# Attention, Elu layer and experts on one core: query projections moved up, half of the key-value products in front of the transposes, and another pacing of the side streams

## The chip, the cores and the metric

The kernel runs on one core of one Trainium2 chip. The metric is the device time of one execution in microseconds (us). The time before is the median of three runs. Times inside an execution come from one profiled execution.

## The reference

Three layers follow each other: a linear attention, an Elu MLP and a mixture of four experts.

```python
# q, k, v: (4, 8, 576, 64); phi(x): proj = x @ w_phi; proj -= max|proj| over the features
#                            phi = [exp(proj), exp(-proj)]   (256 features)
kv  = einsum('bhsf,bhsd->bhfd', phi(k), v);  z = sum_s phi(k)
num = einsum('bhsf,bhfd->bhsd', phi(q), kv)
den = einsum('bhsf,bhf->bhs',  phi(q), z) + 1e-6
x   = (num / den) as (2304 tokens, 512)
h   = x @ w_in                       # 512 x 2048
x   = where(h > 0, h, exp(min(h, 0)) - 1) @ w_out
p   = domain_probs / sum(domain_probs)
out = sum_e p[:, e] * (relu(x @ w1[e]) @ w2[e])   # 4 experts, 512 x 1024 x 512
```

## The kernel before, in words

**Streams.** The attention is cut into 16 pairs of heads (4 batches, 4 pairs each). `pair(i)` is a Python generator that is stepped 11 times, and `attention()` steps up to three pairs in turn: a new one begins every 5 steps (`ATT_LAG`), so the second half of a pair runs beside the first half of the next one. A second generator, `weight_stream()`, prepares weights: 32 conversions of the first half of w_in and w_out in SBUF (the ring), 32 conversions of the second half that are written to DRAM, and after them the split weights of the next stage, which it calls phase -1.

**A pair, in the order of its matmuls (with the names of the tables below).** L233 projects the last 64 keys. `proj(kt)` (L216, 16 matmuls) projects the keys, and `guard` (L222 the maximum, L223 the subtraction, both on VectorE) writes kp0 and kp1. `kexp` (L226, L227, ScalarE) makes exp and exp of the negative. `proj(qt)` and two more guards write qd0 and qd1. `tpose` (L262) transposes the guarded queries, four blocks a call, alternately from qd0 and qd1, and `qexp` (L270) writes their exponentials to ew. `kv` (L255, L256) multiplies the exponentials of the keys with the values. kvw (L284) is the copy of the result. `den` (L319) gives the denominator, copied to dd (L320, ScalarE). A DMA on ScalarE's queue (L325) spreads it to dn, VectorE adds 1e-6 and inverts (L331, L332), a DMA on SyncE's queue writes rec (L333), and two more read it back broadcast as rb (L337). `num` (L309) gives the numerator nd. L340 on VectorE multiplies nd with rb, and `put_x` writes the halves xh (L293, ScalarE) and xl (L296, GpSimd), which the Elu layer reads.

**The next pair's inputs.** `load(i+1)` (L171 to L179, SyncE's queue) stands behind the first query guard: kq, wbd in the first pair, v, and behind these six raw weight blocks (`ring_load`, L376) as long as there are any of the 32 left. There is one kq buffer.

**The Elu layer.** Nine tiles t of 256 tokens, four units u. L518 to L520 are its first matmuls (12 before the first `slot()`), L547 to L549 its second. The first two tiles run interleaved in two halves (the part that the title calls two-half), t2 to t6 one after the other, t7 and t8 interleaved. The first tile needs the four pairs of batch 0, and t2 needs the four of batch 1. `slot()` is called four times a unit: it steps the attention by `rate` and the weights by `wrate`.

**What sets the order.** Each engine has one queue, run in order. A list scheduler fixes the queues ahead of the run by its own estimate of what is ready; the order of the code is only its priority. Steps that a generator emits earlier are thus offered earlier, and can still be placed behind others.

**Phase -1 and the experts.** The second half of the Elu layer (L645 to L647, L724 to L726) and the four experts (L645 to L749) make up the rest of the span, from 441.6 us on.

Of the kernel before, what the change touches and what calls it, by code (L numbers as in the profile page):

```python
# [43 lines left out]
ATT_LAG = 5  # L44
PRE = 1.2
RATE = 1.4
WRATE = 2
WHEAD = 5
CVB = 4
# [3 lines left out]
HEAD = 2  # L53
SEG = 2
ATE = 6
# [14 lines left out]
def attn_elu_moe_kernel(ctx: ExitStack, tc: tile.TileContext, kq_in, vv, w_phi, w_in, w_out, probs, w1, w2, out):  # L70
# [7 lines left out]
    def pool(name, bufs=1, stack=ctx, **kw):  # L78
        return stack.enter_context(tc.tile_pool(name=name, bufs=bufs, reuse_waits="tile", **kw))
# [104 lines left out]
    def bank(shape=(P, 512)):  # L184
        return psum[0].tile(list(shape), F32, tag="bank", name="bank")
# [9 lines left out]
    for i in range(2):  # L195
        t = a1.tile([P, 10, P], F32, name=f"vt{i}")
# [6 lines left out]
    def blocks(t, n):  # L203
        return t[:, :n * P].rearrange("p (n f) -> p n f", f=P)

    def pair(i):
        b, p = divmod(i, NP)
        kq, v = loaded.pop(i)
        kt, qt = kq[:, :512], kq[:, 640:]

        def proj(src):
            ps = [bank() for _ in range(2)]
            for t in range(4):
                for h in range(2):
                    r = slice(h * D, h * D + D)
                    PE.matmul(blocks(ps[h], 4)[:, t], src[r, t * P:(t + 1) * P], wbd[r, h], start=True, stop=True)  # L216
            return ps

        def guard(dst, ps, n):
            src = blocks(ps, n)  # L220
            mx = a1.tile([P, n, 1], F32, tag=f"mx{n}", name="mx", bufs=2)
            V.tensor_reduce(out=mx[:, :, 0], in_=src, op=ALU.max, axis=AX.X, apply_absolute_value=True)  # L222
            mark[0] = V.tensor_tensor(out=dst, in0=src, in1=mx.to_broadcast([P, n, P]), op=ALU.subtract).ins  # L223

        def kexp(d0, d1, src):
            A.activation(d0, src, ACTF.Exp)  # L226
            amark[0] = A.activation(d1, src, ACTF.Exp, scale=-1.0).ins  # L227
# [10 lines left out]
        yield  # L238
        kexp(kp[0][:, :, 0], kp[0][:, :, 1], kp[0][:, :, 1])
        guard(kp[1][:, :, 1], pk1, 4)  # L240
        yield
        kexp(kpm[:D, :, 0], kpm[:D, :, 1], md[:D])
        kexp(kp[1][:, :, 0], kp[1][:, :, 1], kp[1][:, :, 1])
        pq0, pq1 = proj(qt)
        guard(qd[0], pq0, 4)
        if i + 1 < B * NP:
            loaded[i + 1] = load(i + 1)
        yield
        guard(qd[1], pq1, 4)
        yield  # L250
        pk = bank((P, 4, P))

        def kv(h, c):
            for t in range(4):
                PE.matmul(pk[:, 2 * h + c], kp[h][:, t, c], v[:, 4 * h + t], start=(t == 0), stop=False)  # L255
            PE.matmul(pk[:, 2 * h + c], kpm[:, h, c], v[:, 8 + h], start=False, stop=True)  # L256

        def tpose(j):
            pt = bank()
            for t in range(2):  # L260
                for h in range(2):
                    PE.transpose(blocks(pt, 4)[:, 2 * h + t], qd[h][:, 2 * j + t], ident)  # L262
            return pt
# [3 lines left out]
        def qexp(ps, c0, n):  # L267
            src = ps[:, :512].rearrange("p (h s) -> p h s", h=2)[:, :, :n] if n > P else blocks(ps, 2)[:, :, P - n:]
            for c, sc in ((0, 1.0), (1, -1.0)):
                amark[0] = A.activation(ew[:, :, c, c0:c0 + n], src, ACTF.Exp, scale=sc).ins  # L270

        kvw = a1.tile([P, 4, P], F32, tag=("kvh", "kvl")[i % 2], name="kvw")
        qexp(tpose(0), 0, 256)
        kv(0, 0)
        kv(0, 1)
        yield
        qexp(tpose(1), 256, 256)
        pt = bank()
        for h in range(2):
            PE.transpose(pt[:, h * P:(h + 1) * P], md[:, h], ident)  # L280
        qexp(pt, 512, D)
        kv(1, 0)
        kv(1, 1)
        A.activation(kvw, pk, ACTF.Copy)  # L284
# [60 lines left out]
    def attention():  # L345
        live = []
        nxt = 0
        step = 0
        while nxt < B * NP or live:
            if nxt < B * NP and step % ATT_LAG == 0:  # L350
                live.append(pair(nxt))
                nxt += 1
            for g in list(live):
                if next(g, True):
                    live.remove(g)
                    done[0] += 1
                else:
                    yield
            step += 1
# [52 lines left out]
    ready = set()  # L412
# [82 lines left out]
    def need_w(key):  # L495
        while key not in ready:
            next(weights, None)
# [4 lines left out]
    HU = FP // 2  # L502
# [87 lines left out]
    def split_x(g, load_half, keep):  # L590
        xs = [None] * 7

        def put(k, d):
            xv = xb.tile([P, 2, 2, TC], F32R, tag="xv", name="xv", bufs=XV)
            A.activation(xv[:, 0], d, ACTF.Copy)  # L595
            on[XL[k]].tensor_tensor(out=xv[:, 1], in0=d, in1=f32(xv[:, 0]), op=ALU.subtract)  # L596
            if keep:
                SP.dma_start(xvd[g][k], f32(xv))
            xs[k] = xv

        def sub(d, x, y):
            V.tensor_tensor(out=d, in0=x, in1=y, op=ALU.subtract)

        b22 = load_half(g, 1, 1)
        b12 = load_half(g, 1, 0)
        b11 = load_half(g, 0, 0)
        yield
        t0 = xb.tile([P, 2, TC], F32, tag="xt", name="xt", bufs=1)
        put(0, b11)
        sub(t0, b22, b12)  # L610
        yield
        sub(b12, b12, b11)
        put(1, t0)
        b21 = load_half(g, 0, 1)
        yield
        put(6, b22)
        put(3, b12)
        yield
        sub(b22, b22, b12)
        put(2, b21)  # L620
        yield
        put(4, b22)
        sub(b21, b21, b22)
        put(5, b21)
        xcur[0] = g, xs
# [138 lines left out]
    def slot():  # L764
        quota[0] += rate[0]
        while quota[0] >= 1:
            quota[0] -= 1
            if done[0] < limit[0]:
                next(stream, None)
        wquota[0] += wrate[0]  # L770
        while wquota[0] >= 1:
            wquota[0] -= 1
            next(weights, None)

    wrate = [WHEAD]
    wquota = [0.0]
    quota = [0.0]
    rate = [0.0]
# [3 lines left out]
    def drive(unit):  # L782
        unit.l1(slot)
        pend.append(unit)
        if len(pend) > LAG:
            pend.pop(0).l2(slot)

    def order(tail):
        seq = [(t, u) for k in range(0, HU, SEG) for t in range(HEAD) for u in range(k, k + SEG)]
        return seq + [(t, u) for t in range(HEAD, NTS - tail) for u in range(HU)] + [(t, u) for u in range(HU) for t in range(NTS - tail, NTS)]  # L790
# [8 lines left out]
    for t, u in order(TAIL):  # L799
        if u == 0:  # L800
            goal = NP * ((TS * t + TS - 1) // S + 1)
            while done[0] < goal:
                next(stream)
            limit[0] = NP * (t // 2 + 2)
            rate[0] = RATE if t < ATE else 0.0
            if t == HEAD:
                wrate[0] = WSLOW
            if t == ATE:
                att.close()
                xb = pool("xb")  # L810
                wst[0] = pool("wst")
                cmp = pool("cmp")
                wrate[0] = WFAST
            if t == NTS - TAIL:
                nxt = split_x(0, x_att, False)
        need_w(("elu", u))
        drive(Elu(t, u))
        next(nxt, None)
    for _ in nxt:
        pass  # L820
    wrate[0] = WRATE
    need_w(("w1", -1, 0))
# [176 lines left out]
```

## Time and profile before

| | |
|---|---|
| time, median of 3 runs | 1403.98 us (1400.96 to 1405.23) |
| profiled execution | 1403.51 us |
| its span | 1401.4 us |
| mean clock granted to TensorE | 0.989 |
| busy: TensorE, weight loads, VectorE, ScalarE, GpSimd | 1360.0, 1235.3, 661.0, 603.3, 365.3 us |
| first matmul of the Elu layer, first of phase -1 | 88.3 us, 441.7 us |

The span is the time between the first and the last instruction of the trace; 2.1 us of the profiled execution lie outside it. TensorE is busy for 97% of the span. Its busy time depends on the granted clock, so a matmul at half clock counts twice the time. The first 88 us hold the four pairs of batch 0 with nothing of the Elu layer between them.

### The profile page before, as it was taken

Reading aid. Unit: us, or ns where it says so; the run is one execution under the profiler, and the core shown is the slowest. Engines: PE = TensorE matmul, PEld = TensorE weight load, DVE = VectorE, ACT = ScalarE, POOL = GpSimd, SP = SyncE. Lnnn points to the kernel's source line nnn. Section 1 sums busy time; section 2 is a strip of 40 time slices with the busy share of each in tenths; the row PEclk is TensorE's granted clock in tenths of the full one; section 3 lists DMA queues with packets and bytes.
Section 4 is the critical chain, followed back from the end, with each engine's and each line's share of the span. In section 5 each row is a group of like instructions: output and inputs, shape, how many; then the busy total and the mean of one; then the engine's idle time right before and its main releaser. Section 6 shows DMA issues by size and latency. Waiting matters only on the chain.

```text
span 1401.4 us, 22057 instructions
## 1 busy us (share of the span) xinstructions
PE 1360.0 (97%) x8408; PEld 1235.3 (88%) x8408; DVE 661.0 (47%) x1212; ACT 603.3 (43%) x1347; POOL 365.3 (26%) x433
## 2 busy tenths in 40 slices
PE   6889999999999999999999999999999999999998
PEld 5679788989999999999898888988888988889897
DVE  5667875664543757583433422324333334323232
ACT  4668656564545747473343442124321224321121
POOL 3448753221226102352202430003410014300000
PEclk9999999999999999999999999999999999999999
DMA  7533355431414131464614143343245241433521
GB/s 219 177 97 107 95 184 154 137 113 56 136 46 151 30 113 37 130 222 140 219 63 180 45 143 113 135 158 120 80 143 202 96 166 38 143 128 120 181 68 68
DMA packets 105337, 173.46 MB, mean 124 GB/s; under 512 B 33040, under 2 KB 50576, under 8 KB 105232
## 3 DMA queue, kind: packets, MB, share of 16 engines
q1 hardware_dynamic: 98224, 162.55, 35.8%
q10 hardware_dynamic: 7008, 9.51, 1.9%
q8 instruction: 66, 1.08, 0.3%
q14 instruction: 39, 0.32, 0.1%
HBM read 118.13 MB, written 53.81 MB: 123 GB/s over the span
## 4 chain that ended last, share of the span: by engine, by line
PE 86%; DMA 6%; DVE 3%; ACT 2%; issue 1%; POOL 1%; SPq 1%; DVEq 0%; ACTq 0%; POOLq 0%
PE bank L645 9%; PE bank L647 9%; PE bank L646 9%; PE bank L747 9%; PE bank L748 9%; PE bank L749 9%; PE bank L255 3%; PE bank L518 3%; PE bank L547 2%; PE bank L520 2%; PE bank L519 2%; PE bank L548 2%; PE bank L549 2%; PE bank L724 2%; PE bank L725 2%; PE bank L726 2%
## 5 line engine op out<-in xcount | busy, mean ns | idle before, releaser
L645 PE MATMUL bank<-xv,w 128*128 128x384 f32 x840 | 279.1, 337 | 4.0 <-DVE c L659 1.6
L646 PE MATMUL bank<-xv,w 128*128 128x384 f32 x840 | 282.1, 336 | 0.0
L647 PE MATMUL bank<-xv,w 128*128 128x384 f32 x840 | 278.5, 336 | 0.0
L747 PE MATMUL bank<-w,h 128*128 128x512 f32 x576 | 225.8, 395 | 2.3 <-ACT h L661 2.3
L748 PE MATMUL bank<-w,h 128*128 128x512 f32 x576 | 227.4, 395 | 0.0
L749 PE MATMUL bank<-w,h 128*128 128x512 f32 x576 | 202.6, 395 | 0.0
L477 POOL TENSOR_TENSOR w<-wst,w 128x256 fp32r<-128x256 f32 x100 | 78.8, 793 | 389.5 <-ACT w L476 264.0
L645 PEld LDWEIGHTS bank<-xv,w 128*128 128x128 f32 x840 | 157.8, 188 | 13.4 <-DVE c L659 2.6
L646 PEld LDWEIGHTS bank<-xv,w 128*128 128x128 f32 x840 | 158.0, 188 | 4.8
L647 PEld LDWEIGHTS bank<-xv,w 128*128 128x128 f32 x840 | 157.6, 188 | 0.0
L747 PEld LDWEIGHTS bank<-w,h 128*128 128x128 f32 x576 | 108.2, 188 | 25.1 <-ACT h L661 3.0
L662 DVE SCALAR_TENSOR_TENSOR h<-bank,h 128x384 fp32r<-128x384 f32 x144 | 76.9, 554 | 112.9 <-ACT h L661 112.7
L748 PEld LDWEIGHTS bank<-w,h 128*128 128x128 f32 x576 | 108.2, 188 | 23.0
L661 ACT ACTIVATE h<-bank 128x384 fp32r<-128x384 f32 x144 | 66.7, 489 | 141.7 <-PE bank L647 90.0
L749 PEld LDWEIGHTS bank<-w,h 128*128 128x128 f32 x576 | 107.5, 188 | 21.4 <-DVE h L662 0.3
L651 ACT ACTIVATE cmab<-bank 128x384 f32<-128x384 f32 x60 | 29.4, 490 | 182.9 <-PE bank L647 182.9
L596 POOL TENSOR_TENSOR xv<-xs,xv 128x768 fp32r<-128x768 f32 x24 | 45.9, 1916 | 185.9 <-ACT xv L595 179.5
L659 DVE TENSOR_TENSOR bank<-cm,bank 128x384 f32<-128x384 f32 x48 | 26.9, 561 | 126.5 <-PE bank L647 112.6
L518 PE MATMUL bank<-xh,w 128*128 128x256 f32 x288 | 84.1, 292 | 2.3 <-ACT xh L293 2.0
L547 PE MATMUL bank<-gh,w 128*128 128x256 f32 x288 | 84.5, 295 | 0.0
L519 PE MATMUL bank<-xl,w 128*128 128x256 f32 x288 | 81.3, 282 | 0.3 <-POOL xl L296 0.3
L548 PE MATMUL bank<-gl,w 128*128 128x256 f32 x288 | 81.5, 283 | 0.0
(116 smaller groups left out, 2601.2 us busy)
## 6 DMA issues: line engine op xcount, KB each, us to landing
xv<-xvd SPq DMA_DIRECT2D x42, 768.0 KB, 4.1
wst<-in_w SPq DMA_DIRECT2D x64, 256.0 KB, 2.7
xvd<-xv SPq DMA_DIRECT2D x21, 768.0 KB, 4.3
yscr<-y SPq DMA_DIRECT2D x54, 256.0 KB, 2.6
y<-yscr SPq DMA_DIRECT2D x54, 256.0 KB, 3.1
kq<-in_kq SPq DMA_DIRECT2D x16, 320.0 KB, 3.3
rb<-rec SPq DMA_DIRECT2D x32, 144.0 KB, 3.0
xscr<-nd ACTq DMA_DIRECT2D x16, 288.0 KB, 2.0
```

The source lines that it names most:

```text
L477: on[WL[v % len(WL)]].tensor_tensor(out=lo, in0=x, in1=f32(hi), op=ALU.subtract)
L518: PE.matmul(ph[:, j], w[:, 0, c], xh[:, kc], start=(kc == j == 0), stop=False)
L519: PE.matmul(ph[:, j], w[:, 0, c], xl[:, kc], start=False, stop=False)
L547: PE.matmul(o, w[:, 0, c], self.gh[:, j], start=start, stop=False)
L548: PE.matmul(o, w[:, 0, c], self.gl[:, j], start=False, stop=False)
L645: PE.matmul(o, hi[:, c], x[:, 0, kc], start=not more and kc == 0, stop=False, skip_group_check=more)
L646: PE.matmul(o, hi[:, c], x[:, 1, kc], start=False, stop=False, skip_group_check=more)
L647: PE.matmul(o, lo[:, c], x[:, 0, kc], start=False, stop=kc == 1, skip_group_check=more)
L662: V.scalar_tensor_tensor(out=h[:, 1], in0=c, scalar=0.0, in1=f32(h[:, 0]), op0=ALU.max, op1=ALU.subtract)
L747: PE.matmul(self.acc, h[:, 0, c], w[0], start=f == 0, stop=False)
L748: PE.matmul(self.acc, h[:, 0, c], w[1], start=False, stop=False)
L749: PE.matmul(self.acc, h[:, 1, c], w[0], start=False, stop=f == 2 * NQ - 1)
```

## The change

Four edits. (1) `proj(qt)` is emitted one step earlier, right behind the second key guard. (2) `kv(0, 0)` and `kv(0, 1)`, the products with kp0, are emitted ahead of the first `tpose`, behind the second query guard. The number of steps of a pair stays 11. (3) While t is 0 or 1, a slot steps the attention 2.0 times on average, not 1.4 times. (4) A slot doesn't step the weights while `wrate` is 5 and the last ring unit is converted. `wrate` is 5 (`WHEAD`) until t2 begins; it is 5.0 (`WFAST`) again from t6 to the end of the Elu layer, where `need_w` alone then steps the weights, all that are wanted at once.

```diff
+RHEAD = 2.0
...
         kexp(kp[0][:, :, 0], kp[0][:, :, 1], kp[0][:, :, 1])
         guard(kp[1][:, :, 1], pk1, 4)
+        pq0, pq1 = proj(qt)
         yield
         kexp(kpm[:D, :, 0], kpm[:D, :, 1], md[:D])
         kexp(kp[1][:, :, 0], kp[1][:, :, 1], kp[1][:, :, 1])
-        pq0, pq1 = proj(qt)
         guard(qd[0], pq0, 4)
...
         guard(qd[1], pq1, 4)
-        yield
         pk = bank((P, 4, P))
...
+
+        kv(0, 0)
+        kv(0, 1)
+        yield
 
         def tpose(j):
...
         qexp(tpose(0), 0, 256)
-        kv(0, 0)
-        kv(0, 1)
         yield
...
-        wquota[0] += wrate[0]
+        if wrate[0] != WHEAD or ("elu", HU - 1) not in ready:
+            wquota[0] += wrate[0]
...
-            rate[0] = RATE if t < ATE else 0.0
+            rate[0] = RHEAD if t < HEAD else RATE if t < ATE else 0.0
```

The lines of the changed kernel stand one higher from L216 on, four higher at L262 and two higher from L280 on.

**Place 1: TensorE, the third pair, before the Elu layer.** Before:

```order
L216 MATMUL bank<-wbd,kq 128x128 x8
L319 MATMUL bank<-ew,kvw 32x288 x8
L309 MATMUL bank<-ew,kvw 64x288 x8
L216 MATMUL bank<-wbd,kq 128x128 x8
L262 MATMUL bank<-ident,qd_506 128x128
L255 MATMUL bank<-vt_216,kp_503 128x128 x4
L256 MATMUL bank<-vt_216,kpm 128x128
L255 MATMUL bank<-vt_216,kp_503 128x128 x4
L256 MATMUL bank<-vt_216,kpm 128x128
```

The first L216 row is the keys' projection, the second the queries'; L319 and L309 belong to the pair before; kp_503 and kp_504 are kp0 and kp1, qd_506 and qd_507 are qd0 and qd1. Of the change:

```order
L217 MATMUL bank<-wbd,kq 128x128 x8
L321 MATMUL bank<-ew,kvw 32x288 x8
L217 MATMUL bank<-wbd,kq 128x128 x8
L311 MATMUL bank<-ew,kvw 64x288 x8
L255 MATMUL bank<-vt_216,kp_503 128x128 x4
L256 MATMUL bank<-vt_216,kpm 128x128
L255 MATMUL bank<-vt_216,kp_503 128x128 x4
L256 MATMUL bank<-vt_216,kpm 128x128
L255 MATMUL bank<-vt_216,kp_504 128x128
L266 MATMUL bank<-ident,qd_506 128x128
```

The queries' projection now stands ahead of the numerator, and the products with kp0 stand ahead of the first transpose.

**The same pair on VectorE.** Before:

```order
L222 TENSOR_REDUCE mx<-bank 128x4 x2
L223 TENSOR_TENSOR qd_506<-bank,mx 128x512
L331 TENSOR_SCALAR dn<-dn 128x9
L223 TENSOR_TENSOR qd_507<-bank,mx 128x512
L124 TENSOR_SCALAR pcs<-pcs 128x256
L332 RECIPROCAL dn<-dn 128x9
```

These are the query guards, with the L331 of the pair before between them. Of the change:

```order
L223 TENSOR_REDUCE mx<-bank 128x4 x2
L127 SCALAR_TENSOR_TENSOR top<-raw,pcs 128x256
L224 TENSOR_TENSOR qd_506<-bank,mx 128x512
L333 TENSOR_SCALAR dn<-dn 128x9
L224 TENSOR_TENSOR qd_507<-bank,mx 128x512
L128 TENSOR_SCALAR raw<-top 128x256
L334 RECIPROCAL dn<-dn 128x9
```

Nothing has moved between the two guards: qd1 stands behind L333 (L331 before), as it did.

**Place 2: TensorE, where t1 ends and t2 begins.** Before:

```order
L549 MATMUL bank<-gh,w 128x256
L216 MATMUL bank<-wbd,kq 128x128 x8
L262 MATMUL bank<-ident,qd_2128 128x128
L255 MATMUL bank<-vt_216,kp_2125 128x128 x4
L256 MATMUL bank<-vt_216,kpm 128x128
L255 MATMUL bank<-vt_216,kp_2125 128x128 x4
L256 MATMUL bank<-vt_216,kpm 128x128
L255 MATMUL bank<-vt_216,kp_2126 128x128 x2
L262 MATMUL bank<-ident,qd_2129 128x128
```

This is the end of the Elu layer's work on t1; then, in one go, the pair of qd_2128, and behind it the first L518 of t2. Of the change:

```order
L551 MATMUL bank<-gh,w 128x256
L217 MATMUL bank<-wbd,kq 128x128 x4
L311 MATMUL bank<-ew,kvw 64x288 x8
L551 MATMUL bank<-gh,w 128x256
L255 MATMUL bank<-vt_216,kp_1905 128x128 x4
L256 MATMUL bank<-vt_216,kpm 128x128
L255 MATMUL bank<-vt_216,kp_1905 128x128 x4
L256 MATMUL bank<-vt_216,kpm 128x128
L520 MATMUL bank<-xh,w 128x256
```

The same pair (its queries are qd_1908 here) now lies among matmuls of the Elu layer: behind these rows, twelve matmuls L520 to L522 stand ahead of its first transpose.

**Place 3: ScalarE, near the end of the Elu layer, t7, second unit.** Before:

```order
L526 ACTIVATE g_5049<-bank_5024 128x512
L527 ACTIVATE g_5049<-g_5049 128x512
L530 ACTIVATE gh_5050<-g_5049 128x512
L476 ACTIVATE w_5148<-wst_4649 128x256
L476 ACTIVATE w_5151<-wst_4649 128x256
L476 ACTIVATE w_5154<-wst_4647 128x256
L526 ACTIVATE g_5114<-bank_5089 128x512
```

The rows of gh are the Elu layer's own; the rows of w are splits of the weights of phase -1. Of the change:

```order
L528 ACTIVATE g_4992<-bank_4967 128x512
L529 ACTIVATE g_4992<-g_4992 128x512
L532 ACTIVATE gh_4993<-g_4992 128x512
L478 ACTIVATE w_5393<-wst_5374 128x256
L478 ACTIVATE w_5396<-wst_5374 128x256
L478 ACTIVATE w_5399<-wst_5372 128x256
L528 ACTIVATE g_5057<-bank_5032 128x512
```

The scheduler has put the splits in the same place, though the code emits them only behind the last unit.

## Rows read from the trace of the kernel before

**Rows 1.** Busy time by stretches of the span: start:end, length, then each engine.

```profile
0.00:88.30 88.30, 64.72 (x549) 54.29 (x550) 51.23 (x111) 48.11 (x124) 32.51 (x53) 0.90 0.60 183
...
175.00:213.00 38.00, 35.22 (x280) 31.32 (x282) 28.64 (x69) 21.77 (x56) 20.25 (x30) 0.91 0.62 192
213.00:441.60 228.60, 228.60 (x2009) 212.01 (x2006) 122.13 (x222) 124.84 (x276) 70.59 (x91) 1.00 0.35 105
```

**Rows 2.** TensorE's waits before 88.3 us: line, releaser, total, times, longest.

```profile
PE bank L262 <- DVE qd L223: 13.2, 4, 5.0
...
PE bank L262 <- ACT w L152: 2.1, 1, 2.1
```

**Rows 3.** TensorE in short stretches: length, busy, granted clock.

```profile
30.00:33.40 3.40, 3.40 (x19) 0.50 0.27 96
...
176.80:180.10 3.30, 3.30 (x18) 0.50 0.70 197
```

**Rows 4.** TensorE's timeline, 21.5 to 47 us: start, us, what, idle before.

```profile
22.95 1.18 PE L319 MATMUL bank<-ew,kvw 128*32 128x288 f32 x16
...
26.14 1.16 PE L216 MATMUL bank<-wbd,kq 64*128 64x128 f32 x16
29.37 0.30 PE L262 MATMUL bank<-ident,qd 128*128 128x128 f32 x1 [2.06 <-DVE qd L223]
...
33.34 0.63 PE L233 MATMUL bank<-wbd,kq 128*128 128x256 f32 x2
...
37.11 1.16 PE L216 MATMUL bank<-wbd,kq 64*128 64x128 f32 x16
39.62 1.18 PE L319 MATMUL bank<-ew,kvw 128*32 128x288 f32 x16 [1.35 <-ACT kvw L284]
```

**Rows 5.** VectorE's timeline, 21.5 to 32 us.

```profile
22.94 1.29 DVE L222 TENSOR_REDUCE mx<-bank 128x4 f32<-128x512 f32 x2 [2.22 <-PE bank L216]
...
28.54 0.68 DVE L223 TENSOR_TENSOR qd<-bank,mx 128x512 f32<-128x512 f32 x1
29.98 0.68 DVE L331 TENSOR_SCALAR dn<-dn 128x9 f32<-128x9 f32 x1 [0.76 <-DMA dn<-dd]
...
30.91 0.68 DVE L223 TENSOR_TENSOR qd<-bank,mx 128x512 f32<-128x512 f32 x1
```

**Rows 6.** ScalarE's timeline, 23 to 30 us.

```profile
24.64 1.10 ACTq L325 DMA_DIRECT2D dn<-dd  x1
...
27.43 0.63 ACT L227 ACTIVATE kp<-kp 128x512 f32<-128x512 f32 x1
```

**Rows 7.** TensorE's timeline, 10 to 21 us, the first pair.

```profile
13.06 0.45 PE L262 MATMUL bank<-ident,qd 128*128 128x128 f32 x1 [4.08 <-DVE qd L223]
```

**Rows 8.** VectorE's timeline, 32 to 40 us and 60 to 76.6 us.

```profile
37.28 0.76 DVE L340 TENSOR_TENSOR nd<-nd,rb 128x576 f32<-128x576 f32 x1 [0.98 <-DMA rb<-rec]
...
73.69 0.76 DVE L340 TENSOR_TENSOR nd<-nd,rb 128x576 f32<-128x576 f32 x1 [6.00 <-DMA rb<-rec]
```

**Rows 9.** SyncE's queue, 14 to 46 us: the DMA issues.

```profile
22.62 2.01 SPq L376 DMA_DIRECT2D raw<-in_w_out  x4
...
27.37 0.33 SPq L171 DMA_DIRECT2D kq<-in_kq  x1
```

**Rows 10.** The page: DMA issues, KB each, median us from issue to landing.

```profile
kq<-in_kq SPq DMA_DIRECT2D x16, 320.0 KB, 3.3
```

**Rows 11.** TensorE's waits, 88.3 to 213 us.

```profile
PE bank L262 <- DVE dn L331: 3.1, 1, 3.1
PE bank L518 <- ACT xh L293: 2.0, 1, 2.0
```

**Rows 12.** Groups by line and shape, 213 to 441.6 us: count, busy us, mean ns.

```profile
L131 POOL TENSOR_TENSOR top<-top,w 128x256 f32<-128x256 f32 x17 | 12.6, 742 | 1.1
...
L124 DVE TENSOR_SCALAR pcs<-pcs 128x256 f32<-128x256 f32 x16 | 6.8, 425 | 2.7 <-ACT pcs L120 2.7
```

**Rows 13.** The page: a costly group, the weight splits of GpSimd.

```profile
L477 POOL TENSOR_TENSOR w<-wst,w 128x256 fp32r<-128x256 f32 x100 | 78.8, 793 | 389.5 <-ACT w L476 264.0
```

## The prediction

> **What bounds the kernel now.** I read the stretches first, to see where TensorE isn't busy; then its waits, for what it lacks there; then the timelines, for what each wait hangs on. From 213 to 441.6 us TensorE is busy for the whole 228.60 us, with VectorE, ScalarE and GpSimd at 122, 125 and 71 us [rows 1]: nothing is to be won there, and other engines have room. Two stretches have gaps: before 88.3 us it is busy for 64.72 us at a mean granted clock of 0.90, and between 175 and 213 us for 35.22 of 38.00 us at 0.91 [rows 1]. In the first, the wait that counts is that of the first transpose (L262): 13.2 us in four waits, which end when qd is written, and one of 2.1 us of the same kind [rows 2]. These are five pairs, the four of batch 0 and the next one. Behind a wait the granted clock is often 0.50, the lower of the two levels (1.2 GHz): 30.0 to 33.4 us is one of four such stretches before 88.3 us [rows 3]. What runs there takes twice as long, so the 3.40 us of the first hold 1.70 us of work. Near t2 there are two waits, 3.1 and 2.0 us [rows 11], and two half-clock stretches, of which 176.8 to 180.1 us is one [rows 3]. The rest of the span, from 441.6 us on, is code that the change doesn't touch.
>
> **The first edits before the Elu layer (A).** A cycle is the time from one denominator (L319) to the next: 22.95 to 39.62 us, so 16.67 us [rows 4]. In it TensorE waits 2.06 us at the first transpose and 1.35 us for kvw, and 1.70 us are lost to the half clock, 5.1 us in all [rows 3, 4]. The change puts the queries' projection ahead of the numerator, so it can start behind the denominator, at 24.13 (22.95 + 1.18), and not at 26.14: 2.0 us earlier. And it gives TensorE the products with kp0 to do, ahead of the transpose, since the key exponentials are done at 28.06 (27.43 + 0.63) [rows 6] and the projections at 27.30 (26.14 + 1.16) [rows 4]: a wait of under 1 us there, not 2.06 at the transpose, and the transposes find qd0 written.
>
> That isn't the whole of it, since the transposes alternate between qd0 and qd1. In the order of VectorE, L331 stands between the two guards, before and after. It waits for the DMA dn, which starts from the denominator of the pair before: it begins at 29.98, 7.03 us behind the start of L319, and qd1 is written at 31.59 (30.91 + 0.68) [rows 5]. Moving the queries' projection up doesn't move this. So I cost the cycle as a chain: 8.64 us from L319 to qd1 (31.59 - 22.95); then what stands between the second transposes and the next projection, L233 at 33.34 to L216 at 37.11, 3.8 us [rows 4]; then from there to the next denominator 2.51 us (39.62 - 37.11), projection and wait for kvw. The sum is 14.9 us, 1.7 us under 16.67. The products with kp0 lie beside the 8.64 us and cost nothing; without that cover, they would add at full clock half of the 4.0 us from 29.37 to 33.34, which is nearly all theirs at half clock: 2.0 us. There are three such cycles: 5.2 us. The first pair has no denominator in front of it, and waits 4.08 us [rows 7]; there the products (2.0 us) fill part of the wait: 2 us. The last pair, with the wait of 5.0 us, is late for another reason: in the cycle before, L340 held VectorE's queue for 6.00 us until rb had landed [rows 8], with key and query guards behind it. I give this 0. **A is -7 us.** The lower bound is a chain that has grown (second rival), 0; the upper one is that all four cycles go at TensorE's own pace, 16.67 - 5.1 + 1.3 (kvw) = 12.9 us, 11.4 us in three of them and 2 in the first pair, -13 us; I take the value by the chain of rows, since each link is measured.
>
> **The boundary to t2 (B).** Now the catch-up before t2 runs eleven attention steps in one go. With 2.0 steps per slot all are issued by then, and the last pair of batch 1 lies among the matmuls of t1 (place 2: twelve matmuls of the Elu layer are ahead of its first transpose). The waits of 3.1 and 2.0 us and the half-clock losses of 2 x 1.65 us (half of 3.30) [rows 3, 11] make 8.4 us. The price is none on TensorE, whose matmuls are the same: before 175 us it is busy nearly all the time, and steps done earlier only move. L518 still needs xh, which comes behind dn, rec, rb and L340; what is left between the last denominator and the first L518 of t2 is some 24 us of matmuls by my count in the order, and the whole way from a denominator to its L340 is 14.3 us in the cycle above (22.95 to 37.28) [rows 4, 8]. So I take most of it: **B is -7 us**, between -3 (only the first wait goes) and -8.4.
>
> **The conversions (C).** The pause ends the conversions during t0 and t1 when the 32 of the ring are done, and 20 of the 32 that go to DRAM, done by t2 before, are now issued in t2 to t6, 2.2 steps a slot. Each is two operations on GpSimd (at most 742 ns each), four on VectorE (425 ns as the first of them) and two on ScalarE [rows 12]: 20 x 1.5 = 30 us more on GpSimd and 20 x 1.7 = 34 us more on VectorE in a stretch where they have 158 and 106 us free [rows 1]. TensorE waits for nothing there, and gl, which VectorE or GpSimd writes, is read two units later. Bounds: 0, and the 2 to 3 us of a handful of small waits. I take +1.
>
> **The weights at the end of the Elu layer (D).** `wrate` is 5.0 again from t6 on, which equals `WHEAD`, so the pause also stops the weights of phase -1 until `need_w` after the last unit. In the order (place 3) the scheduler has put the splits back into t7, beside the same rows of gh. So D is +0.5 us, for the last conversions among them, with bounds 0 and what the fourth rival costs.
>
> The sum goes against the profiled execution: 1403.5 - 7 - 7 + 1 + 0.5 = 1391.0 us. It is 0.5 us below the median of the runs, which changes nothing. About 4.2 us (0.3%) is what a measurement of this kernel can tell from no change.
>
> **The rivals.** *Second: the DMA chain grows.* There is one kq buffer, and the load of the next pair, now at 27.37 us, waits for the queries' projection. If that ends 2.0 us earlier, the load starts at about 25.4, beside the issue of dn (24.64 to 25.74) [rows 6, 9], and takes 3.3 us to land [rows 10]. In front of dn there are already raw blocks, issued from 22.62 on [rows 9]. If dn lands 2 to 3 us later, the cycle is 17 to 18 us, and A is +0 with the first pair: 1403.5 - 7 + 1.5 = 1398 us. For it speaks that dn takes 5.3 us from its issue to L331 now (24.64 to 29.98); against it, that its issue still comes before that of kq.
> The Trainium skill has a rule that speaks for this rival ("DMA: Bandwidth & Descriptors", section "Queues, rings and completion order"): a DMA's semaphore increment lands only behind every earlier write of the same DMA engine, across its queues. By that rule a small transfer behind large ones pays for them, and the late dn behind the raw blocks agrees [rows 5, 9]; whether kq gets in front of it, no row shows.
>
> *Third: nearly all goes.* If dn lands earlier, or the scheduler's place for L331 costs nothing, A is -13 and B -8.4, C and D nothing: 1382 us. Against it stands the row of L331.
>
> *Fourth: the weights are late (D).* If the splits run only behind the last unit, 28 of L477 (four units of seven) at 0.79 us [rows 13] are 22 us on GpSimd, of which the first seven, 5.5 us, stand in front of the first matmul of phase -1, and the others in front of those that follow: +8 to +14 us, 1399 to 1405 us, no change that can be measured or little. The order speaks against it.
>
> *Fifth, the other side: the products wait for the key exponentials where nothing waited.* In t2 to t6 eight pairs run among the Elu layer's matmuls, without a wait now [rows 1]. There too the products with kp0 stand ahead of the transposes now. They need the exponentials on ScalarE, 5.1 us behind the start of the key guards (22.94 to 28.06) [rows 5, 6], and ScalarE has the conversions of C in its queue. If each of the eight waits 1.5 us and loses 1.7 us to the half clock behind it, that is 26 us: 1391 + 26 = 1417 us. It decides from 1.75 us a pair on (14 / 8); above that the kernel is slower than before. Against it: a pair's steps lie far apart there, with Elu matmuls between, which the scheduler puts in front of what isn't ready.
>
> **How the numbers follow.** The forecast (A, B, C and D as above) has 0.55, at 1391 us, with a range of its own of 1386 to 1395 us. The second rival has 0.15 (1398), the third 0.12 (1382), the fourth 0.09 (1399 to 1405), the fifth 0.09 (from 1408 on). Faster by over 0.3% (below 1399.8): 0.55 + 0.12 and nearly all of the second, 0.82. Within 0.3%: the fourth, 0.09. Slower: the fifth, 0.09. The range from 1381 to 1401 us leaves out the fifth and most of the fourth.
>
> **What the profile after would show.** The first L1 matmul (L520) at about 81 us rather than 88.3, the first of phase -1 at about 428 rather than 441.7, and 960 us from there to the end as before. The waits of the transposes for qd in the first part well below 15 us, with those that are left ended by qd1 behind L333; products (L255) waiting under 1 us for key exponentials. No wait of over 1 us and no half clock near t2. No waits between t2 and t6. Wrong is the forecast if the cycles stay above 16 us (second rival), if the first matmuls of phase -1 wait for w (fourth), or if TensorE's waits show L255 in t2 to t6 (fifth).

## The result and the profile after

The change takes 1390.55 us (median of four runs, 1389.05 to 1392.23) against 1403.68 us in the same series: a ratio of 0.9909, with a 95% interval of 0.9896 to 0.9922. The forecast was 1391.0 us. The profiled execution took 1390.87 us, with a span of 1389.1 us and a mean granted clock of 0.996 (0.989 before).

TensorE's busy time by stretches, cut at the first matmul of the Elu layer (78.4 us) and the first of phase -1 (428.9 us); the columns are start:end, length, busy time, granted clock, DMA share and GB/s:

```profile
0.00:78.40 78.40, 62.08 (x550) 0.96 0.69 206
78.40:213.00 134.60, 134.60 (x1201) 1.00 0.33 102
213.00:428.80 215.80, 214.53 (x1838) 1.00 0.39 117
428.80:453.80 25.00, 21.21 (x113) 0.93 0.48 146
```

Beside [rows 1]: the idle time in the first stretch has fallen from 23.6 to 16.3 us; the gap near t2 is gone, and with it the low clock there; and there is now 1.3 us of idle time between t2 and t6, where there was none. The waits of TensorE over the whole span, largest first:

```profile
PE bank L321 <- ACT kvw L286: 4.7, 3, 2.2
PE bank L234 <- DMA wbd<-in_w_phi: 4.2, 1, 4.2
PE bank L234 <- DMA kq<-in_kq: 3.3, 1, 3.3
PE bank L255 <- ACT kp L227: 2.9, 1, 2.9
PE bank L647 <- ACT cmab L653: 2.8, 1, 2.8
...
PE bank L550 <- DVE gl L533: 0.6, 1, 0.6
PE bank L549 <- ACT gh L532: 0.5, 1, 0.5
PE bank L266 <- DVE qd L224: 0.3, 1, 0.3
```

The 13.2 + 2.1 us of [rows 2], in which the first transpose waited, are 0.3 us now (last row), and the waits of [rows 11] have gone. What stands in their place is smaller: kvw (3.4 us before, of which [rows 4] show one), the load of kq (0.8 us before), the products with kp0 once (2.9 us), and cmab at the entry of phase -1 (2.8 us). Where the time went, stage by stage:

| stage | before | after | difference | forecast |
|---|---|---|---|---|
| up to the first Elu matmul | 88.3 | 78.4 | -9.9 | A, -7 |
| from there to the first matmul of phase -1 | 353.4 | 350.5 | -2.9 | B and C, -6 |
| the rest of the span | 959.7 | 960.2 | +0.5 | D, +0.5 |
| span | 1401.4 | 1389.1 | -12.3 | -12.5 |

The sum is right and the parts aren't: the first stage gave 3 us more, the second 3 us less, and that the two cancel is luck. In the second stage, what TensorE lost before were 5.7 us of idle time [rows 1, with 83.80 of 86.70 us busy between] and 3.3 us of half clock [rows 3]; after, 1.3 us of idle time. That is 7.7 us less, yet the stage is only 2.9 us shorter. TensorE thus does 5 us more in it, with the same matmuls. The groups by line and shape show which, first of before from 88.3 to 441.6 us, then of the change from 78.4 to 428.8 us (count, busy us, mean ns of one):

```profile
L216 PE MATMUL bank<-wbd,kq 64*128 64x128 f32 x352 | 26.1, 285 | 0.0
```

```profile
L217 PE MATMUL bank<-wbd,kq 64*128 64x128 f32 x352 | 31.2, 285 | 0.0
```

The same 352 matmuls of the projections, 285 ns each, take 5.1 us more. The timeline of the change shows how, in one of the pairs that run beside t2 to t6:

```profile
265.68 1.16 PE L217 MATMUL bank<-wbd,kq 64*128 64x128 f32 x16
...
269.69 1.16 PE L217 MATMUL bank<-wbd,kq 64*128 64x128 f32 x8
...
271.57 1.16 PE L217 MATMUL bank<-wbd,kq 64*128 64x128 f32 x8
```

A projection's sixteen matmuls alternate between two heads, whose operands lie in partitions 0 to 63 and 64 to 127, and take 1.16 us. The queries' projection of this pair is cut in two by the scheduler: eight matmuls of one head, 1.9 us later eight of the other, and each half takes as long as a whole one. Four projections of the trace are cut so (at 145, 221, 270 and 313 us) and one in three pieces (at 83 us), by the order that the scheduler has fixed.
The Trainium skill bears on this ("TensorE: Matmul & The Clock Gate", section "Part 3: Packing small matmuls — row/col tiling"): matmuls on different rows of the array run beside each other, in the order in which they are issued. The rows here agree: 16 in 1.16 us in turn, 8 in 1.16 us apart.

### The profile page after: what moved, and what is told of

It reads as the page before. It is cut to its first block, busy times and chain, and to the rows that moved or that the text cites. A ratio compares the mean times of both kernels' runs of the same rounds, so it can differ in the third digit from the quotient of the medians.

```text
span 1389.1 us, 22035 instructions
## 1 busy us (share of the span) xinstructions
PE 1358.5 (98%) x8408; PEld 1234.0 (89%) x8408; DVE 659.0 (47%) x1212; ACT 603.2 (43%) x1347; POOL 365.3 (26%) x433
## 4 chain that ended last, share of the span: by engine, by line
PE 82%; DMA 6%; DVE 3%; ACT 2%; POOL 2%; issue 2%; SPq 0%; ACTq 0%; DVEq 0%; POOLq 0%
PE bank L647 9%; PE bank L649 9%; PE bank L648 9%; PE bank L749 9%; PE bank L750 9%; PE bank L751 9%; PE bank L255 3%; PE bank L217 2%; PE bank L726 2%; PE bank L727 2%; PE bank L728 2%; PE bank L520 2%; PE bank L549 2%; PE bank L521 2%; PE bank L522 2%; PE bank L550 2%
## 5 line engine op out<-in xcount | busy, mean ns | idle before, releaser
L520 PE MATMUL bank<-xh,w 128*128 128x256 f32 x288 | 84.4, 293 | 0.0
```

The source lines that it names most:

```text
L520: PE.matmul(ph[:, j], w[:, 0, c], xh[:, kc], start=(kc == j == 0), stop=False)
```

## The experiments

All compute the same as the change. Each has its ratio to the kernel before, timed beside it; the change stands at 0.9909. Stages are those of the table above, for the change 78.4, 350.5 and 960.2 us.

**The order alone.** Edits 1 and 2, without 3 and 4:

```diff
-            rate[0] = RHEAD if t < HEAD else RATE if t < ATE else 0.0
+            rate[0] = RATE if t < ATE else 0.0
-        if wrate[0] != WHEAD or ("elu", HU - 1) not in ready:
-            wquota[0] += wrate[0]
+        wquota[0] += wrate[0]
```

> Edits 1 and 2 alone (projection up, products in front of the transposes); 1.4 steps per slot and no pause, as before. My theory: the two edits of the order carry the whole gain before the Elu layer (about 11 us of waits and half clock), and only part of that at t2, since the catch-up of eleven steps stays there: the transposes' wait goes, the wait for xh stays, so 4 to 5 us of 9. Against that stand projections that the scheduler cuts in two by head (six of them whole, in this order), at about 1.08 us each: +6. Time about 1395 us, first Elu matmul at 78 to 79 us, one wait for xh near t2. Rival, the order carries everything: 1390 to 1391 us. Rival, the order carries only what I forecast for A: 1397 us or more.

Measured: 1393.14 us, 0.992 (0.9903 to 0.9937). That is between my theory and the first rival, with the first Elu matmul at 75.9 us, earlier than I expected: the order carries most of the gain. The stretches before and behind the first Elu matmul:

```profile
0.00:75.90 75.90, 60.94 (x549) 1.00 0.71 208
75.90:428.90 353.00, 351.38 (x3037) 1.00 0.37 112
```

1.6 us of idle time are left in the second one, and no half clock: the order alone takes the waits at t2, which I had put down to the catch-up. But TensorE is busy for 351.4 us there, since the cut projections take 32.3 us, not 26.1.

**The pacing alone.** Edits 3 and 4 on the kernel before.

> Edits 3 and 4 alone (2.0 steps per slot for t0 and t1, the pause), with the order of a pair as before. My theory: nothing changes before the first Elu matmul (88 us), both waits and both half-clock stretches near t2 go (9 us), the moved conversions cost about 1 us, no projection is cut: 1395 to 1396 us. Rival, the steps that are issued earlier wait for their own transposes among the Elu matmuls, since qd1 is late there too: waits of 1 to 3 us in t0 and t1 and 1399 to 1403 us.

Measured: 1397.84 us, 0.996 (0.9944 to 0.9976), between theory and rival. The theory's mechanism holds: the first Elu matmul is at 90.0 us (88.3 before), and the second stage is 346.2 us, 7.2 us shorter than before, with the projections at 25.6 us. The remaining waits in it are 3.2 us, 1.0 of them for dn. So both halves of the change can take the waits at t2, and their gains (11 and 6 us) don't add up to more than 13.

**The heads kept in turn.**

```diff
-            for t in range(4):
-                for h in range(2):
-                    r = slice(h * D, h * D + D)
-                    PE.matmul(blocks(ps[h], 4)[:, t], ...)
+            def one(t, h):
+                r = slice(h * D, h * D + D)
+                return PE.matmul(blocks(ps[h], 4)[:, t], ...).ins
+
+            one(0, 0)
+            with tc.issue_after(one(0, 1)):
+                for t in range(1, 4):
+                    for h in range(2):
+                        one(t, h)
```

> The changed kernel with each projection's sixteen matmuls kept in the alternation of the two heads: the third and all later ones must be placed behind the first one of the second head. Nothing else. In the trace of the change four projections are cut in two halves by head, and each half takes 1.08 us, as much as a whole projection that alternates (1.09 us). My theory: that is a loss of 4.3 us on TensorE and some 0.6 us for those cut in other ways, which comes back: 1385 to 1386 us, no projection over 1.2 us. Rival, the halves ran where TensorE would have had nothing else to do, or the other half now waits for its bank: 1390 to 1391 us.

Measured: 1389.72 us, 0.9895 (0.9878 to 0.9911): not told apart from the change. The projections' busy time in the second stage falls by half of the excess, and the rows show why not by all:

```profile
268.51 0.48 PE L216 MATMUL bank<-wbd,kq 64*128 64x128 f32 x2
...
270.43 1.16 PE L216 MATMUL bank<-wbd,kq 64*128 64x128 f32 x14
```

```profile
L216 PE MATMUL bank<-wbd,kq 64*128 64x128 f32 x352 | 28.7, 287 | 0.0
```

The first pair of matmuls still goes ahead by itself, and by the row this costs 0.48 us. The first matmul of phase -1 comes at 426.7 us, 2.2 us earlier than in the change; the rest then takes 962.7 us, 2.5 us more. In its first 33 us TensorE waits twice for 2.4 us:

```profile
PE bank L652 <- ACT cmab L658: 2.4, 1, 2.4
PE bank L731 <- ACT h L709: 2.4, 1, 2.4
```

**Every projection head by head.**

```diff
-            for t in range(4):
-                for h in range(2):
+            for h in range(2):
+                for t in range(4):
```

> The changed kernel with every projection emitted head by head (four tokens blocks of the first head, then four of the second) and not in turn. It measures what the cut costs by itself. My theory: a half of one head alone takes as long as both heads in turn, so each of the 32 projections that is not cut now costs up to 1.08 us more: if no two halves overlap, 28 x 1.08 = 30 us, 1420 us; if halves that stand next to each other overlap partly, half of that, 1405 us. Rival, heads in turn give nothing: 1390 to 1391 us.

Measured: 1402.65 us, 0.9987 (0.9976 to 0.9999), 12 us above the change: the second of the two prices, halves that stand next to each other overlap partly. In its second stage the projections take 39.2 us:

```profile
L217 PE MATMUL bank<-wbd,kq 64*128 64x128 f32 x352 | 39.2, 285 | 0.0
```

That is 8.0 us over the change and 13.1 over the kernel before, and the stage as a whole is 8.0 us longer than in the change. This shows the price by itself: which matmuls alternate is worth as much as the whole change.

**One edit of the order at a time.** First the projection alone (edit 1):

```diff
         guard(kp[1][:, :, 1], pk1, 4)
+        pq0, pq1 = proj(qt)
         yield
```

> Edit 1 alone: the queries' projection one step earlier; the products with kp0 stay behind the first transposes, pacing as before. My theory: each of the two edits of the order alone removes about two thirds of the waits before the Elu layer, since qd0 comes 2 us earlier and the wait was 2.06 us, but qd1 stays behind dn and nothing stands between. A -7, t2 -5, cut projections (four whole) +4: about 1396 us. Rival a: this edit is all of it, 1393 us as with both. Rival b: the products are all of it, and this edit alone gives 1401 to 1404 us.

Measured: 1397.15 us, 0.9953 (0.993 to 0.9976). Then the products alone (edit 2), with the projection where it was:

> Edit 2 alone: the products with kp0 in front of the transposes; the queries' projection where it was, pacing as before. My theory: the products fill most of the wait for qd, but start 0.75 us late for the key exponentials (28.06 against 27.30): A -7, t2 -4, fewer cut projections, +2: about 1395 us. Rival a: 1393 us as with both. Rival b: the projection's place is all of it, and this alone gives 1401 to 1404 us.

Measured: 1398.18 us, 0.9956 (0.9939 to 0.9973). The times are about as my theory had them, the split by stages is not. The stretches before and behind the first Elu matmul, of the projection alone:

```profile
0.00:81.10 81.10, 62.19 (x549) 0.94 0.67 199
81.10:431.40 350.30, 348.08 (x3037) 1.00 0.37 112
```

and of the products alone:

```profile
0.00:75.90 75.90, 63.70 (x549) 0.98 0.70 209
75.90:434.70 358.80, 349.35 (x3037) 1.00 0.37 111
```

The products alone bring the first Elu matmul to 75.9 us, as early as both edits do, but leave 9.5 us of idle time behind it; the largest part, 3.3 us in two waits, is for w, the converted weights. The projection alone leaves four waits of 1.0 to 3.0 us at the transposes in the first stage, besides the 4.1 us of the first pair, and 2.2 us of idle time in the second. Both edits shorten the first stage, the products by 12.4 us and the projection by 7.2; in the second, only the earlier projection gains (3.1 us), and the products alone lose 5.4.

**The pause ended at t6**, with the heads kept in turn:

```diff
-        if wrate[0] != WHEAD or ("elu", HU - 1) not in ready:
+        if wst[0] is not None or wrate[0] != WHEAD or ("elu", HU - 1) not in ready:
```

> The kernel with the heads kept in turn (the third run), and the pause ended when t6 begins, so that the weights run on from there at 5 steps a slot. In that run and in the change the last three conversions lie on ScalarE and GpSimd at the entry of phase -1 and TensorE waits there 3.8 to 5.0 us, against 2.6 before. My theory: that is the price of the pause in its second part, 1 to 2 us, and it goes: 1388 us, and a wait for cmab under 1 us. Rival: the entry is bound by the weights themselves, which the scheduler puts in the same place, 1389 to 1390 us and the same waits.

Measured: 1393.56 us, 0.9931 (0.9903 to 0.9958); no gain. The wait for cmab falls as expected, but others come:

```profile
PE bank L555 <- DVE gl L538: 2.5, 1, 2.5
PE bank L652 <- DVE c L703: 2.0, 1, 2.0
...
PE bank L652 <- ACT cmab L658: 0.6, 1, 0.6
```

On VectorE, a weight conversion (L126 to L128, 2.3 us) now stands in front of gl, which is written at 371.0 us, and TensorE waits 2.5 us there, where the change waits 0.6. The price has moved, not gone. This profile also tells how far one profile can be trusted: up to the first Elu matmul it has the same order on every engine as the third experiment, and reaches it at 75.7 us instead of 78.5, with 1.3 us of wait for kq instead of 2.5 and one half-clock stretch less.

**The projection one step earlier still**, right behind the first key guard, heads in turn:

```diff
         guard(kp[0][:, :, 1], pk0, 4)
+        pq0, pq1 = proj(qt)
         yield
         kexp(kp[0][:, :, 0], kp[0][:, :, 1], kp[0][:, :, 1])
         guard(kp[1][:, :, 1], pk1, 4)
-        pq0, pq1 = proj(qt)
```

> The kernel with the heads kept in turn, and the queries' projection one step earlier still, right behind the first key guard, so that it stands ahead of the denominator, where TensorE now waits for kvw (4.7 us in three waits). My theory: it fills these waits, and frees kq earlier: -3 us, 1386 to 1387 us, the first Elu matmul at 75 us. Rival: it doesn't fill them, because the four banks of both projections are held at once and the next matmuls wait for a bank, or because the query guards now stand ahead of work that is wanted first: 1389 to 1393 us.

Measured: 1391.52 us, 0.9914 (0.9886 to 0.9942): the rival's time, and only in part for its reason. The rows show 0.7 us of waits for a bank that a guard still reads, as the rival had it, and a wait of 2.3 us for qd. Yet the first matmul of phase -1 comes at 424.1 us, 4.8 us earlier than in the change and 2.6 earlier than in the kernel with the heads in turn, with the wait for kvw down to 3.0 us; the rest of the span takes 964.8 us, 4.6 us more than in the change. Part of this is the entry of phase -1, where 4.3 us are idle in the first 25 us (3.8 in the change, 2.6 before), and part a half-clock stretch at 1198.5 us that the change's profile doesn't have:

```profile
424.10:449.10 25.00, 20.73 (x108) 0.93 0.48 143
```

**Pause and rate apart.** Without the pause:

> The change without the pause (edits 1, 2 and 3). The two edits of the order alone gave 1393.1 us, all four 1390.6. My theory: the pause gives nothing by itself and costs 1 to 3 us at the entry of phase -1, where the last conversions hold ScalarE's queue; so without it 1388 to 1390 us, with no wait for cmab of over 1 us there. Rival: the pause is what gives the last 2.5 us, since the conversions otherwise stand in ScalarE's and VectorE's queues during t0 and t1: 1393 us.

Measured: 1392.79 us, 0.9906 (0.9884 to 0.9927), the same ratio as the change: the pause gives nothing and costs nothing that can be measured. The profiled execution is the fastest of the six here (1386.55 us). In it, the wait for cmab at the entry of phase -1 is 0.6 us, but there is one of 1.7 us for c. With the pause and 1.4 steps per slot:

> The change with 1.4 steps per slot for t0 and t1 as before (edits 1, 2 and 4). My theory: the order has already taken the waits at t2 (1.6 us are left), so 2.0 steps per slot bring little, and fewer cut projections at most: 1392 to 1394 us. Rival: the rate carries what the order alone lacks and the pause costs nothing: 1392.5 to 1393.5 with the same entry wait as the change, or, if the rate itself costs (pairs crowded into t0 and t1), under 1390 us.

Measured: 1395.46 us, 0.993 (0.9912 to 0.9947), by the ratio as my theory had it (1393.9 us beside the change's 1390.6); its second stage is 354.0 us. With both edits of the order in place, the rate is worth about 3 us (0.993 against 0.9909 of 1404), not resolved beyond the intervals.

**Heads in turn, without the pause.**

> Edits 1, 2 and 3, with the heads of each projection kept in turn, no pause. My theory: the 2.6 us that the kept turn won on TensorE before phase -1 were lost again at its entry, behind conversions that the pause had made late; without the pause both gains stand: 1386 to 1388 us, the best so far. Rival: the entry waits for the weights whenever TensorE arrives earlier, pause or not: 1389 to 1391 us.

Measured: 1393.51 us, 0.9903 (0.9879 to 0.9928): by the ratio, the rival (1390.1 us). The entry of phase -1 still waits, for h and for c, without the pause. The runs of before in this series lie between 1399 and 1409 us, so the ratio is what counts.

**The product with rb one step later**, on the change:

```diff
         yield
+        yield
         with tc.issue_after(mark[0]):
             V.tensor_tensor(out=xf, in0=nd, in1=rb, op=ALU.mult)
```

> The change with the product of numerator and rb (L342 there) one step later, behind one more yield of the pair, so that it stands between the two key guards on VectorE and not ahead of both. In the change it waits 4.8 us for rb in the last cycle before the Elu layer, with the key guards behind it, and TensorE then waits 2.9 us for the key exponentials and loses 1.4 us to the half clock. My theory: rb's DMA, through that one instruction, is what is left of the last pair's lateness: without it in front of kp0's guard the 2.9 us and the half clock go, the first Elu matmul comes at 74 to 76 us instead of 78.4, and the time is 1387 to 1389 us on the scale of the change's 1390.6. Rival: the same instruction now holds kp1's guard and xh comes later, so the wait only moves: a wait of 2 to 4 us at products with kp1 or at the first Elu matmuls, and 1390 to 1393 us.

Measured: 1387.84 us, 0.9889 (0.9871 to 0.9907), the lowest ratio of all; the intervals of this and of the change still overlap. VectorE's timeline in the last cycle before the Elu layer, first of the change:

```profile
68.73 0.76 DVE L342 TENSOR_TENSOR nd<-nd,rb 128x576 f32<-128x576 f32 x1 [4.79 <-DMA rb<-rec]
69.40 0.68 DVE L224 TENSOR_TENSOR kp<-bank,mx 128x512 f32<-128x512 f32 x1
...
70.34 0.68 DVE L224 TENSOR_TENSOR kp<-bank,mx 128x512 f32<-128x512 f32 x1
```

and of this kernel:

```profile
65.14 0.68 DVE L224 TENSOR_TENSOR kp<-bank,mx 128x512 f32<-128x512 f32 x1
65.74 0.75 DVE L343 TENSOR_TENSOR nd<-nd,rb 128x576 f32<-128x576 f32 x1
66.40 0.69 DVE L224 TENSOR_TENSOR kp<-bank,mx 128x512 f32<-128x512 f32 x1
```

The 4.8 us of waiting for rb are gone. But the place on VectorE isn't what took them away in this cycle, since rb lands earlier. SyncE's queue shows why, first of the change:

```profile
58.82 1.81 SPq L378 DMA_DIRECT2D raw<-in_w_in  x4
60.72 0.86 SPq L378 DMA_DIRECT2D raw<-in_w_out  x2
61.66 1.10 SPq L339 DMA_DIRECT2D rb<-rec  x2
```

and of this kernel:

```profile
55.84 0.92 SPq L379 DMA_DIRECT2D raw<-in_w_out  x2
...
61.32 1.18 SPq L339 DMA_DIRECT2D rb<-rec  x2
```

In the change, six raw weight blocks of 256 KB are issued right in front of rb, and rb is there at 68.7 us, 6.5 us behind the start of its second issue. With the extra step, the scheduler has put the blocks earlier, and by the trace's semaphore records rb has landed at 65.2 us, 3.3 us behind its second issue. The first guard starts at 65.14 us, so in front of it L343 would have waited for next to nothing too. What the step on VectorE gives without the other order of the loads, no run shows. TensorE's waits up to the first Elu matmul have no L255 behind kp any more:

```profile
PE bank L321 <- ACT kvw L286: 5.3, 4, 2.8
PE bank L234 <- DMA wbd<-in_w_phi: 4.2, 1, 4.2
PE bank L234 <- DMA kq<-in_kq: 3.4, 1, 3.4
PE bank L266 <- DVE qd L224: 1.0, 1, 1.0
PE bank L255 <- issue: 1.0, 1, 1.0
```

The first Elu matmul is still at 78.4 us, against my expectation, but one more projection and a denominator stand ahead of it (582 matmuls, not 550), and phase -1 begins at 424.7 us, 4.2 us earlier than in the change.

## Why the prediction was right, and where its terms were off

**A, right in direction, 3 us too small, and its chain held one cycle of three.** In the change, from one denominator to the next:

```profile
36.68 1.18 PE L321 MATMUL bank<-ew,kvw 128*32 128x288 f32 x16 [1.34 <-ACT kvw L286]
...
44.82 0.87 PE L266 MATMUL bank<-ident,qd 128*128 128x128 f32 x6 [0.25 <-DVE qd L224]
...
50.98 1.18 PE L321 MATMUL bank<-ew,kvw 128*32 128x288 f32 x16 [2.18 <-ACT kvw L286]
```

and on VectorE, L333 still stands between qd0 and qd1 and waits for dn:

```profile
44.00 0.17 DVE L333 TENSOR_SCALAR dn<-dn 128x9 f32<-128x9 f32 x1 [1.31 <-DMA dn<-dd]
44.08 0.68 DVE L224 TENSOR_TENSOR qd<-bank,mx 128x512 f32<-128x512 f32 x1
```

From the denominator to L333 it is 7.32 us (7.03 before [rows 4, 5]), to qd1 8.1 (forecast 8.64), and the whole cycle is 14.3 us (forecast 14.9). But that chain held only this cycle, and TensorE waits 0.25 us for qd in it: in the one before, both query guards were done before L333, and the one after is 12.8 us (50.98 to 63.77), which is what I had given as TensorE's own pace, 12.9. The three together gained 6.7 us, not 5.2. I had also taken 16.67 us for each of them, where the rows before have 16.67, 16.36 and 14.95 us; they are 14.2, 14.3 and 12.8 us now. What TensorE waits for in each of the three is kvw. In the cycle above, the copy to kvw stands on ScalarE behind the exponentials of the queries, and these behind a weight conversion that waits for GpSimd, though the transposes are done at 45.7 us:

```profile
46.51 0.42 ACT L153 ACTIVATE w<-top 128x256 fp32r<-128x256 f32 x1 [2.89 <-POOL top L132]
46.83 1.06 ACT L274 ACTIVATE ew<-bank 128x512 f32<-128x512 f32 x2
...
50.31 0.61 ACT L286 ACTIVATE kvw<-bank 128x512 f32<-128x512 f32 x1
```

No run moved that conversion, so what it costs stays open. The first pair gained 0.5 us, not 2: the next load's wait (kq, 3.3 us) took the place of the transposes' 4.1 us [rows 7]. And the last pair, which I gave 0, gained 2.8 us (14.6 us from the last denominator to the first Elu matmul, against 17.4): L342 still holds VectorE until rb lands, 4.8 us instead of 6.0 [rows 8], but the products need only the key guards behind it, no longer the query guards too. My sign that the products would wait under 1 us for the key exponentials failed there: they wait 2.9 us. In the last experiment, where rb lands in time, that wait and the half clock behind it are gone.

**B, the step that was mis-sized.** I had "the price is none on TensorE, whose matmuls are the same". The waits and the half clock went, all 9.0 us of them rather than 7; but the matmuls, though the same, are not as fast when the scheduler cuts a projection in two. That is the 5.1 us of the second stage. I had looked at the order of the change for what stands ahead of what, and not for which matmuls stand next to each other. The head-by-head kernel shows the price; that the change would have gained it with whole projections is not shown, since the kernel with the heads in turn won 2.2 us before phase -1 and lost them behind it. My attribution to edit 3 holds for the pacing alone, which shortens the stage by 7.2 us and leaves 3.2 us of idle time; but in the change it isn't needed for that, since the order alone leaves 1.6.

**C, right.** +1.3 us of idle time, 1.1 of it the two waits for gl and gh at 367 us. No product with kp0 waits between t2 and t6, so the fifth rival fell.

**D, right in size, with another mechanism beside it.** The splits of the weights are where the order had them, and the rest of the span is 0.5 us longer. That this agrees to a tenth is luck: from one kernel's profile to the next, the rest takes between 959.7 and 964.8 us with the same matmuls. The wait for cmab (2.8 us) is ScalarE's queue, where its copy stands behind splits of w_out's half:

```profile
440.41 0.63 ACT L490 ACTIVATE w<-wst 128x512 fp32r<-128x512 f32 x1 [2.76 <-POOL w L491]
441.75 0.63 ACT L490 ACTIVATE w<-wst 128x512 fp32r<-128x512 f32 x1 [0.71 <-DMA wst<-wout]
442.29 0.47 ACT L653 ACTIVATE cmab<-bank 128x384 f32<-128x384 f32 x1
```

Before, the waits at this place were 1.6 and 0.8 us. Both kernels with TensorE earlier at this point wait more there, with the pause and without; I take the entry to be bound by the weights' splits on ScalarE and GpSimd, but no run moved those alone, so that stays open.

**The second rival fell.** In the cycle above, kq's load is issued at 39.02 us, ahead of dn at 39.57, so that it does get in front. Behind its issue, dn is used after 4.4 us (44.00 - 39.57), not later than the 5.3 us before, when four raw blocks stood right in front of it [rows 5, 6, 9]; behind the denominator, it is used 0.3 us later than before and not 2 to 3, since its issue comes 2.9 us behind the denominator and not 1.7.

## What to carry to other kernels

Cost a pipelined loop by its chain, link by link from the rows, and check each cycle by itself, since another link may hold the next one. When a change lets a scheduler place work more freely, look in the order for matmuls that run beside each other only when they stand next to each other: with the same instructions, busy time can grow. An instruction that waits for a DMA in an engine's queue costs what stands behind it. Ask first what that DMA itself waits behind; here, the large loads issued in front of it decided when it landed.

## What the runs showed of the hardware

Two heads' matmuls of 64 rows take 1.16 us for sixteen in turn and 1.16 us for eight of one head alone. Sixteen emitted head by head next to each other cost less than two halves apart: the projections of a stage took 26.1 us nearly all in turn and 39.2 us nearly all head by head, 0.6 us more for each of the 22. A transfer behind large ones lands late: the two DMAs of rb (144 KB each) were there 6.5 us behind the start of the second issue with six blocks of 256 KB right in front of them, and 3.3 us without. And one half-clock stretch more or less goes with small differences: two executions with the same order reached the same matmul at 75.7 and 78.5 us.
